# Emitting the five instruction streams directly instead of inside a block scope

## The chip, the cores and the metric

The kernel runs on one core of a Trainium2 chip. The metric is the device time of one execution in microseconds. It is a little longer than the span that the profile shows, which goes from the first to the last instruction of the program: the runtime's own work around the program counts in the time and not in the span. This document calls the difference "time minus span". Spans are listed to 0.1 us, so a single value carries up to 0.05 us of rounding. The means do not depend on it much, and for profiled runs the trace gives the span to a nanosecond.

## The reference, cut to what matters

Two branches on the same normalised input are added to that input: a diagonal state-space layer (a projection in, a complex recurrence over 2048 time steps, a projection out) and a dense layer with a Mish activation.

```
x = A_x                                  # 1 x 2048 x 1024, bf16
xn = layernorm(x)
return x + ssm(xn, Lambda, B, C, log_dt, Dskip) + mish(xn @ w1 + b1) @ w2     # w1: 1024 x 3584
```

The change touches none of this arithmetic.

## The kernel before

The kernel records every operation in one of five queues, one for each engine, with the semaphore waits that it needs. At the end the queues are emitted. An operation is emitted as its waits, then the instruction, which increments a semaphore:

```
    def emit(self, engine):
        known = {}
        for fn, waits, sem, inc in self.items:
            for ev in waits:
                if known.get(id(ev.sem), 0) < ev.val:
                    known[id(ev.sem)] = ev.val
                    engine.wait_ge(ev.sem, ev.val)
            if fn is not None:
                fn(engine).then_inc(sem, inc)
```

The last work of the program is an addition on DVE and an output transfer that ACT issues. SP (SyncE) waits for all output transfers, and this is the last entry of its queue:

```
            vop(lambda e: e.tensor_tensor(xr, src, xr, op=ALU.add), reads=b_src + [b_x], writes=[b_x])
            ...
            out_events[i, q, lo] = AC.dma(lambda e: e.dma_start(out[0, r0:r0 + P, lo:hi], xr), sem, reads=[b_x])
    ...
    SP.wait(out_events.values())

    with nc.Block() as block:
        @block.gpsimd
        def _(eng):
            PO.emit(eng)
        ...                                   # the same for vector, scalar, tensor
        @block.sync
        def _(eng):
            SP.emit(eng)
```

The block scope puts each engine's instructions into a block of its own, with a branch into it and a branch out of it, and ends with a barrier of all engines: each engine drains and counts up one semaphore, POOL waits for the four others and releases them through a second one. A barrier of the same kind stands at the program's start. That one belongs to the program's frame and not to the block.

## Time and profile before

| | before |
|---|---|
| time, median of 6 runs (range) | 624.51 us (624.31 to 625.04) |
| span of the profiled run | 622.4 us |
| PE busy | 616.7 us, 99% |
| time minus span, 25 runs of before with the later experiments | 1.99 us (1.94 to 2.02) |

From the page of the kernel before: the span, the busy time of each engine, and the chain of work that ended last, by engine and by line.

```profile
span 622.4 us, 7441 instructions
...
PE 616.7 (99%) x2981; PEld 287.9 (46%) x2981; DVE 464.1 (75%) x684; ACT 246.7 (40%) x162; POOL 50.2 (8%) x47
...
PE 98%; DMA 1%; DVE 1%; ACT 0%; SPq 0%; issue 0%
PE ps L715 49%; PE ps L638 29%; PE ps L658 18%; PE ps L492 2%; DMA xx<-in_A_x_dram 1%; DVE mt L663 0%; PE ps L378 0%; ACT sq L349 0%; SPq L287 0%; DVE xx L752 0%; ACT xnT L389 0%; DVE xn L366 0%; ACT mv L351 0%; ACT rs L360 0%; DVE rs L365 0%
```

The chain is matmuls for 98% of the span, and what lies after the last addition, 2.2 us of the span and about 2.0 us outside it, is 0.7% of the time. No more than that can be won at the program's end. The next lines are the end of the program in the timeline (start, length, engine, line, operation):

```profile
618.89 1.64 ACTq L754 DMA_DIRECT2D out_dram<-xx  x2
619.46 0.69 DVE L752 TENSOR_TENSOR xx<-ps,xx 128x512 bf16<-128x512 f32 x1 [0.60 <-PE ps L715]
```

The last addition on DVE ends at 620.15 us, but the span ends at 622.4. The views of the profile leave out drains, semaphores and branches, so for these 2.2 us one has to read the raw records of the trace. Here they are for the kernel before (start in us, length in ns; line 131 is the wait in `emit`, line 820 the block):

```
620.183   339 ns  ACT   DMA issue, the last output transfer   L754
621.893           last of the 16 landing counts of that transfer
621.910    28 ns  SP    semaphore wait, last of its queue but one  L131
621.977    41 ns  SP    compare-and-branch, carries the last wait  L820
622.158    13 ns  SP    drain                                 L820
622.196    17 ns  POOL  gathers four engines                  L820
622.274    17 ns  POOL  releases them                         L820
622.327    51 ns  PE    leaves; 622.378 is the end of the span  L820
```

So 0.485 us of the span lie after the last landing. After the span the records show updates of semaphore 2. The Trainium skill ("Runtime: NRT & Kernel Launch", Semaphores 0–2 are reserved) names it as the runtime's sync barrier. There are two passes of nine updates, and between them the user semaphores are set back to zero. In the kernel before, the first pass runs from 0.239 to 1.052 us after the span's end, the resetting ends at 1.604 (623.98 us), and the second pass runs from 1.859 to 2.215.

### The profile page before, as it was taken

The page shows a single profiled execution, that of the slowest core. Times are in us where ns is not written, and L with a number is a line of the kernel's source. Part 1 is how long each engine was busy: PE and PEld are TensorE (multiplying, and loading weights), DVE is VectorE, ACT ScalarE, POOL GpSimd, SP SyncE. Part 2 cuts the span into 40 slices and gives each one's busy share as a digit, 9 for nine tenths or more (in the row PEclk, how much of TensorE's full clock was granted, in tenths as well). Part 3 has the DMA queues.
Part 4 walks back from the last instruction along what each step waited for, and adds up shares of the span by engine and source line. Part 5 has one row for each costly group of instructions (what it writes and reads, how often), then busy time and mean ns, then how long its engine had stood idle before and what let it go on. Part 6 is the DMA issues. An engine that isn't in the chain of part 4 may idle for free.

```text
span 622.4 us, 7441 instructions
## 1 busy us (share of the span) xinstructions
PE 616.7 (99%) x2981; PEld 287.9 (46%) x2981; DVE 464.1 (75%) x684; ACT 246.7 (40%) x162; POOL 50.2 (8%) x47
## 2 busy tenths in 40 slices
PE   8999999999999999999999999999999999999998
PEld 7644444444444444444444444444444444444443
DVE  5799999999557599998147759999624856999603
ACT  6679995341069940000008992000001999000000
POOL 1999000000100000000010000000000000000000
PEclk9999999999999999999999999999999999999999
DMA  9999966750364300863055420285204531043001
GB/s 264 235 296 263 213 134 198 191 153 1 128 195 150 135 2 28 205 195 113 17 186 157 148 102 1 89 216 162 77 34 136 168 135 70 0 136 101 1 0 68
DMA packets 124188, 79.41 MB, mean 128 GB/s; under 512 B 48890, under 2 KB 106490, under 8 KB 124154
## 3 DMA queue, kind: packets, MB, share of 16 engines
q1 hardware_dynamic: 120656, 71.58, 42.5%
q10 hardware_dynamic: 2538, 4.21, 1.8%
q0 software_dynamic: 960, 3.15, 1.5%
q8 instruction: 24, 0.39, 0.3%
q14 instruction: 10, 0.08, 0.0%
HBM read 63.19 MB, written 4.19 MB: 108 GB/s over the span
## 4 chain that ended last, share of the span: by engine, by line
PE 98%; DMA 1%; DVE 1%; ACT 0%; SPq 0%; issue 0%
PE ps L715 49%; PE ps L638 29%; PE ps L658 18%; PE ps L492 2%; DMA xx<-in_A_x_dram 1%; DVE mt L663 0%; PE ps L378 0%; ACT sq L349 0%; SPq L287 0%; DVE xx L752 0%; ACT xnT L389 0%; DVE xn L366 0%; ACT mv L351 0%; ACT rs L360 0%; DVE rs L365 0%
## 5 line engine op out<-in xcount | busy, mean ns | idle before, releaser
L715 PE MATMUL ps<-ring,act 128*128 128x512 bf16 x896 | 194.2, 379 | 0.3 <-DVE mt L663 0.3
L638 PE MATMUL ps<-xnT,ring 128*128 128x512 bf16 x848 | 183.7, 379 | 0.0
L616 ACT ACTIVATE act<-hb 128x3584 bf16<-128x3584 bf16 x16 | 50.9, 3183 | 245.5 <-DVE hb L645 245.2
L715 PEld LDWEIGHTS ps<-ring,act 128*128 128x128 bf16 x896 | 87.6, 98 | 106.2 <-DVE mt L663 0.8
L638 PEld LDWEIGHTS ps<-xnT,ring 128*128 128x128 bf16 x848 | 83.0, 98 | 99.9
L645 DVE TENSOR_SCALAR hb<-ps,par 128x512 bf16<-128x512 f32 x112 | 82.8, 747 | 56.3 <-PE ps L638 54.4
L715 PE MATMUL ps<-CT,hT 128*128 128x512 bf16 x512 | 111.2, 379 | 0.0
L658 PE MATMUL ps<-xnT,BT 128*128 128x512 bf16 x512 | 111.2, 379 | 0.0
L663 DVE TENSOR_TENSOR mt<-ps,tab 128x1024 bf16<-128x1024 f32 x64 | 75.3, 1218 | 13.3 <-PE ps L658 11.8
L658 PEld LDWEIGHTS ps<-xnT,BT 128*128 128x128 bf16 x512 | 50.1, 98 | 60.4
L715 PEld LDWEIGHTS ps<-CT,hT 128*128 128x128 bf16 x512 | 50.1, 98 | 60.4
L752 DVE TENSOR_TENSOR xx<-ps,xx 128x1024 bf16<-128x1024 f32 (+1 forms) x17 | 19.5, 1159 | 70.3 <-PE ps L715 70.2
L681 DVE TENSOR_TENSOR_SCAN hT<-cs,qi,hT 128x512 bf16<-128x512 f32 x48 | 58.9, 1267 | 0.0
L618 ACT ACTIVATE act<-act 128x3584 bf16<-128x3584 bf16 x16 | 51.0, 3190 | 0.2
L617 ACT ACTIVATE act<-act 128x3584 bf16<-128x3584 bf16 x16 | 51.0, 3190 | 0.2
L686 DVE TENSOR_TENSOR mt<-hT,tab 128x1024 bf16<-128x1024 bf16 x64 | 41.4, 688 | 1.1
L623 DVE TENSOR_TENSOR act<-act,hb 128x3584 bf16<-128x3584 bf16 x16 | 32.9, 2058 | 1.3 <-ACT act L618 1.3
L287 POOL DMA_DIRECT2D xx<-in_A_x_dram x12 | 6.7, 559 | 254.0 <-DVE xx L752 249.9
L592 ACT ACTIVATE ct<-CT,cs 128x512 f32<-128x512 bf16 x16 | 11.5, 718 | 28.8 <-DVE CT L594 24.5
L617 ACT ACT_TABLE_LOAD x16 | 20.5, 1283 | 0.3
L618 ACT ACT_TABLE_LOAD x16 | 20.5, 1283 | 0.3
L681 DVE TENSOR_TENSOR_SCAN hT<-cs,hT 128x512 bf16<-128x512 f32 x16 | 18.7, 1207 | 0.0
(78 smaller groups left out, 277.2 us busy)
## 6 DMA issues: line engine op xcount, KB each, us to landing
ring<-in_B_w_dram SPq DMA_DIRECT2D x112, 512.0 KB, 3.7
out_dram<-xx ACTq DMA_DIRECT2D x15, 256.0 KB, 2.0
xx<-in_A_x_dram POOLq DMA_DIRECT2D x12, 256.0 KB, 4.1
xx<-in_A_x_dram SPq DMA_DIRECT2D x4, 256.0 KB, 3.6
dsk<-in_A_Dskip_dram SPq DMA_DIRECT2D x1, 256.0 KB, 6.7
out_dram<-xx ACTq DMA_DIRECT2D x2, 128.0 KB, 1.7
xnT<-xn SPq DMA_TRANSPOSE x12, 4.4
BT<-in_A_B_re_dram SPq DMA_TRANSPOSE x8, 5.7
```

Source lines behind the costliest of these rows:

```text
L616: aop(lambda e: e.activation(a, hs, AF.Exp), reads=[b_hb[g % 2]], writes=[b_act[g]])
L617: aop(lambda e: e.activation(a, a, AF.Ln, bias=1.0), reads=[b_act[g]], writes=[b_act[g]])
L618: aop(lambda e: e.activation(a, a, AF.Tanh), reads=[b_act[g]], writes=[b_act[g]])
L623: vop(lambda e: e.tensor_tensor(a, a, hs, op=ALU.mult), reads=[b_act[g], b_hb[g % 2]], writes=[b_act[g]])
L638: PE.mm(lambda e, k=k: e.matmul(ps[:, bank, :], lhsT=wt[:, k, fi * P:(fi + 1) * P], rhs=xnT[:, k, :], start=k == 0, stop=k == NK - 1), rea ...
L645: vop(lambda e: e.tensor_scalar(hb[:, hs, :], ps[:, bank, :], b1(f), None, op0=ALU.add), reads=[b_ps[bank], b_par], writes=[b_hbf[hs]])
L658: PE.mm(lambda e, j=j, ci=ci, k=k, bank=bank: e.matmul(ps[:, bank + ci, :], lhsT=BT[:, ci, j, k, :], rhs=xnT[:, k, :], start=k == 0, stop= ...
L663: vop(lambda e, s=s, u=u, j=j: e.tensor_tensor(mt[:, s, :, :], u, tab[:, s, j, :].unsqueeze(1).to_broadcast([P, 2, TB]), op=ALU.mult), rea ...
L681: vop(lambda e, ci=ci, init=init: e.tensor_tensor_scan(out=hT[:, ci, j, :], data0=cj("r", j).to_broadcast([P, TB]), data1=hT[:, ci, j, :], ...
L686: vop(lambda e, s=s: e.tensor_tensor(mt[:, s, :, :], hT[:, :, j, :], tab[:, s, j, :].unsqueeze(1).to_broadcast([P, 2, TB]), op=ALU.mult), ...
L715: PE.mm(lambda e: e.matmul(ps[:, u, :], lhsT=lhsT, rhs=rhs, start=st_, stop=last), reads=reads, writes=[b_ps[u]], first=st_, last=last)
L752: vop(lambda e: e.tensor_tensor(xr, src, xr, op=ALU.add), reads=b_src + [b_x], writes=[b_x])
```

## The change

The intent is to save the branches and the closing barrier, which the program does not need: SP has waited for every output transfer by then, and the runtime has a barrier of its own.

```diff
-    with nc.Block() as block:
-        @block.gpsimd
-        def _(eng):
-            PO.emit(eng)
...
-        @block.sync
-        def _(eng):
-            SP.emit(eng)
+    PO.emit(nc.gpsimd)
+    VE.emit(nc.vector)
+    AC.emit(nc.scalar)
+    PE.emit(nc.tensor)
+    SP.emit(nc.sync)
```

## The prediction

> **What bounds the kernel.** TensorE. The page shows PE busy 616.7 of a span of 622.4 us (99%) at granted clock 1.000; the chain that ended last is 98% PE. The time, 624.6 us (624.42 to 625.04), is 2.2 us longer than the span: work around the program.
>
> **What the change touches.** By the programs' instruction order, every compute and DMA instruction stays in place. Taken away are ten unconditional branches (into and out of each engine's block) and a closing barrier of five drains and six semaphore instructions. The opening barrier comes from the program, not from the block, and stays.
>
> **Branches: almost nothing.** The trace's raw records hold one branch, on SP at 621.98 us (41 ns; it carries the last semaphore wait); the nine others go to the next instruction and leave no record. At the start SP's release from the opening barrier stands at 0.708 us and its first DMA issue at 0.791, 83 ns later; two waits of SP in a row, without a branch, stand 67 ns apart: at most 16 ns. The Trainium skill ("Advanced Engine Details and Errata", Control Flow Timing) gives about 51 ns for a branch; the 83 ns leave no room for that. The start should not move: first DMA issue at 0.79, first matmul at 1.41.
>
> **Closing barrier: about 0.44 us of the span.** In the records the last output DMA lands at 621.89; SP's last ordinary wait ends at 621.94; branch 621.98; SP's drain 622.16; POOL gathers 622.20 and releases 622.27; the last engine leaves at 622.38, the span's end. Without the barrier SP's last wait ends the program: 622.38 - 621.94 = 0.44 us, all serial after the last DMA, so it counts in full. The other engines come early (DVE's drain ends 620.20, ACT's 620.72) and wait only for SP.
>
> **Outside the span: perhaps another 0 to 0.3 us.** After the span the records show updates of semaphore 2, which the Trainium skill ("Runtime: NRT & Kernel Launch", Semaphores 0–2 are reserved) names as the sync barrier: nine from 622.62 to 623.43, then the user semaphores cleared[...], then nine more from 624.24 to 624.59. The second pass takes 0.36 us, the first 0.81, because some engine comes late. With the change four engines arrive early and only SP late, so the first pass may come nearer to 0.36 (an estimate).
>
> **Sum.** 624.6 - 0.44 - about 0.15 = 624.0 us; -0.1%. The runs of before spread over 0.62 us, as much as the gain, so I give 623.4 to 624.6. Faster by over 2%: 1%; within 2%: 98%; slower by over 2%: 1%.
>
> **What would show it.** Span about 621.9 us instead of 622.4; last record an SP wait, 0.05 us after the last DMA lands; no drains or semaphores at the block's line; busy times, group means, idle times and first microseconds unchanged; PE chain still 98%. First pass of semaphore 2 earlier and shorter; the reset stage as long as before.
>
> **What would make it wrong.** (1) The runtime's end is set by something other than SP's arrival (an instruction block of 8192 bytes is fetched at 624.00): 0, or some tenths either way, since each engine's stream is now shorter. (2) Engines that enter the runtime's end early disturb the last output DMA or SP. (3) The block's barrier did part of the runtime barrier's waiting, and the gain is taken back there. (4) Run-to-run drift of some 0.3 us hides it.

## More of the kernel before

While the first rows are loaded and normalised, TensorE runs 76 dummy matmuls, so that its clock is up when the real work begins:

```
    keep_busy(76)
    ...
    first_apply(0)          # DVE: normalise rows 0..127
    first_transpose(0)      # PE: the first real work, after the dummies in PE's queue
```

## The result

The changed kernel took 623.77 us, median of 6 runs (623.34 to 624.32), against 624.51 us (624.31 to 625.04). The ratio is 0.9986 with a 95% interval of 0.9973 to 0.9999: faster by about 0.14%. Ratios in this document are the mean time of one kernel's fast runs over that of the other's of the same rounds, so they are not quite the ratio of the medians.

From the page of the changed kernel, the lines that answer to those of before:

```profile
span 622.6 us, 7430 instructions
...
PE 617.8 (99%) x2981; PEld 289.3 (46%) x2981; DVE 464.5 (75%) x684; ACT 246.7 (40%) x162; POOL 50.2 (8%) x47
...
PE 99%; DVE 0%; ACT 0%; POOL 0%; issue 0%; POOLq 0%
PE ps L715 48%; PE ps L638 29%; PE ps L658 18%; PE ps L492 2%; PE ps L457 1%; DVE mt L663 0%; PE ps L378 0%; DVE xx L752 0%; ACT xnT L389 0%; POOL ident L325 0%; POOL ident L324 0%; PE ps L500 0%; POOL kon L328 0%; POOLq L838 0%
```

Here is a trap. The profiled run of the changed kernel has a longer span than that of before (622.6 against 622.4), although the change took instructions away. The end of the timeline shows that the changed program was already late before its end came:

```profile
618.83 1.24 PE L715 MATMUL ps<-CT,hT 128*128 128x512 bf16 x5
...
620.11 0.69 DVE L752 TENSOR_TENSOR xx<-ps,xx 128x512 bf16<-128x512 f32 x1 [0.60 <-PE ps L715]
```

The last addition starts at 620.11 us instead of 619.46, so 0.65 us came in earlier. The chain has a clue: line 457, the dummy matmuls, is on it now (1%), and the load of the input is not. The start of the chain in order of time (start, length, what), first before, then after:

```profile
1.72 4.16 DMA xx<-in_A_x_dram
...
7.79 0.56 DVE xn L366
...
9.78 1.03 PE ps L492 x8
```

```profile
1.42 7.11 PE ps L457 x76
8.52 0.45 PE ps L378 x8
...
10.40 1.03 PE ps L492 x8
```

From the timelines, the dummies, the first normalised rows (DVE) and the first transposes (PE, line 378), first before, then after. The chain above counts a group on PE only from the end of the one before it, so it has the transposes at 8.52 us where the timeline has their start, 8.36:

```profile
1.41 5.65 PE L457 MATMUL ps<-ident 128*128 128x128 bf16 x76 [1.41 <-POOL kon L328]
...
6.83 0.55 DVE L366 TENSOR_SCALAR xn<-xx,mv,rs 128x1024 bf16<-128x1024 bf16 x1
...
7.43 0.62 PE L378 MATMUL ps<-ident,xn 128*128 128x128 bf16 x8 [0.36 <-DVE xn L366]
```

```profile
1.41 7.11 PE L457 MATMUL ps<-ident 128*128 128x128 bf16 x76 [1.41 <-POOL kon L328]
...
6.91 0.55 DVE L366 TENSOR_SCALAR xn<-xx,mv,rs 128x1024 bf16<-128x1024 bf16 x1
...
8.36 0.61 PE L378 MATMUL ps<-ident,xn 128*128 128x128 bf16 x8
```

And the durations of the dummy matmuls (min/median/max in ns), before and after:

```profile
L457 PE MATMUL ps<-ident x84: 219/219/311, 1.4 to 9.0; 128*128 128x128 bf16 x84
```

```profile
L457 PE MATMUL ps<-ident x84: 219/314/314, 1.4 to 9.6; 128*128 128x128 bf16 x84
```

In both kernels the dummies begin slow, 107 ns from start to start, and later quicken to 56 ns. In the run of before this happened at 4.11 us, in the run of the changed kernel at 7.19 us. The 76 dummies therefore last 7.11 us instead of 5.65, and the first transposes, which stand behind them in PE's queue, wait for them: they start at 8.36 us, although the first normalised rows were there at 7.45. The first real matmul (line 492, the dense layer) starts at 10.41 instead of 9.78 us.

The Trainium skill ("TensorE: Matmul & The Clock Gate", What's actually happening) says that the matmul clock is released after a busy window, and that the window is free-running, so that the moment varies from run to run. The traces agree that it varies: in the twelve profiles with 76 dummies the clock rose between 4.11 and 7.32 us, and in the ten of them without the block alone between 4.86 and 7.32. Only two of the twelve have the block, and they were early (4.11 and 5.29), so the profiles cannot show that the block has no part in the moment. Over all runs no difference stands out of the noise: the span less its tail after the last landing (measured once for each kernel) is on average 622.18 us in 47 runs without the block and 622.09 in 30 with it, a difference of 0.09 with a standard error of 0.08. From the first real matmul to the last matmul of the program, on the other hand, eleven of the twelve profiles lie between 609.26 and 609.31 us (the other, the run `e5_hold_pe`, at 609.90: at 93.5 us PE waits 0.91 us for DVE there, and 0.31 in the profile of `e7_hold_pool`). So the middle of the program is the same in all kernels but for one such stop. What differs is the start, which is chance as far as these runs can tell, and the end, which is the change.

The end of the changed kernel, from the raw records:

```
620.830   338 ns  ACT   DMA issue, the last output transfer   L754
622.537           last of the 16 landing counts of that transfer
622.554    28 ns  SP    semaphore wait, the last instruction of the program   L131
622.582           end of the span
```

The span's tail after the last landing is 0.045 us instead of 0.485: 0.44 us less. Time minus span fell as well, from 1.99 to 1.43 us (mean of 6 runs, 1.39 to 1.47). The parts, in us from the end of the span, from the updates of semaphore 2:

| | last landing to end of span | first pass: start, end | second pass: start, end | POOL's step in the second pass |
|---|---|---|---|---|
| before | 0.485 | 0.239, 1.052 | 1.859, 2.215 | 0.039 |
| changed | 0.045 | -2.337, 0.283 | 1.069, 1.621 | 0.233 |

From the last landing to the last update it is 2.700 us before and 1.666 us after, 1.03 us less. That is what the change is worth in these two traces. The difference of the mean times of the 6 and 6 runs is 624.62 - 623.76 = 0.85 us; the chance of the start lies on top (the spans of 25 runs of before have a standard deviation of 0.33 us).

### The profile page after: what moved, and what is told of

Read it like the earlier page. It is cut to its first block, busy times and chain, and to the rows that moved or that the text cites. A ratio compares the mean times of both kernels' runs of the same rounds, so it can differ in the third digit from the quotient of the medians.

```text
span 622.6 us, 7430 instructions
## 1 busy us (share of the span) xinstructions
PE 617.8 (99%) x2981; PEld 289.3 (46%) x2981; DVE 464.5 (75%) x684; ACT 246.7 (40%) x162; POOL 50.2 (8%) x47
## 4 chain that ended last, share of the span: by engine, by line
PE 99%; DVE 0%; ACT 0%; POOL 0%; issue 0%; POOLq 0%
PE ps L715 48%; PE ps L638 29%; PE ps L658 18%; PE ps L492 2%; PE ps L457 1%; DVE mt L663 0%; PE ps L378 0%; DVE xx L752 0%; ACT xnT L389 0%; POOL ident L325 0%; POOL ident L324 0%; PE ps L500 0%; POOL kon L328 0%; POOLq L838 0%
```

## The experiments

Theory: the time lost to the closing barrier has two parts. Inside the span it is the branch, drain, gather and release after SP's last wait. Outside the span it is that all engines come to the runtime's own barrier together, whereas without the closing barrier four of them have long been there and only SP is awaited. Rivals: the branches and the block as such; the length of the instruction streams, which moves what the runtime's instructions stand next to; and that the outside part is only noise. All twelve kernels gave the reference's result. The times of before are of the same rounds.

### e1_direct_barrier: the barrier without the block

```diff
     SP.emit(nc.sync)
+    nc.all_engine_barrier()
```

> The changed kernel (direct emission, no block) with one all-engine barrier put back at its end. Theory: the block's branches cost nothing and the barrier costs everything, so this is the kernel before again: time about 624.5 us like before in the same rounds (within 0.2), time minus span back at about 2.0 us (1.4 in the changed kernel), last landing to the end of the span about 0.4 to 0.5 us (0.485 before, 0.045 after). Rival (branches or block scope matter): part of the gain stays, time about 624.1 or less.

Measured: 624.33 us (623.78 to 624.95) against 624.49; ratio 0.9994 (0.9982 to 1.0007). Time minus span is 1.98 us (before 1.99), so the outside part is the barrier's alone. The tail of the span is 0.296 us, between the changed kernel's 0.045 and the 0.485 of before. SP's last wait stands at 622.207 and its drain at 622.272, 65 ns later. In the kernel before, the branch at 621.977 stands between them and the drain comes at 622.158, 181 ns after the branch. So the 0.44 us of span splits into 0.25 us for the barrier (0.296 - 0.045) and 0.19 us for the one branch of SP that carries a wait (0.485 - 0.296). The theory that branches cost nothing fell for that one. The times alone do not resolve 0.19 us.

### e2_hold_all: no barrier, but all five engines wait for the last transfers

```diff
     SP.wait(out_events.values())
+    for held in (PO, VE, AC, PE):
+        held.wait(list(out_events.values())[-2:])
```

> The changed kernel, but POOL, DVE, ACT and PE each also wait at their end for the last two output transfers, as SP does: no barrier, but all five engines reach the runtime's own end together. Theory: the gain outside the span comes from four engines doing their part of the runtime's end early, so it is lost here: time minus span about 2.0 us instead of 1.4, while the span's tail stays short (last landing to the end of the span 0.05 to 0.15 us); time about 0.4 us under before, about 0.6 over the changed kernel. Rival (the outside gain comes from shorter streams or another cause): time minus span stays 1.4 us.

Measured: 624.83 us (624.05 to 624.87) against 624.49; ratio 1.0 (0.9986 to 1.0013). The tail is 0.079 us, as short as expected, and time minus span is 2.08 us. The outside gain is gone without any barrier: it is enough that the engines come late together. The first pass shows it directly: it ends 0.804 us after the span, and 0.283 in the changed kernel. The time itself did not come out 0.4 us under before as expected; ratio and interval do not tell 0.999 from 1. One thing does not add up fully: the last update of semaphore 2 came 1.959 us after the span in this trace, less than the 2.215 of before, while the time minus span of the profiled run is 1.96, nearly the 2.02 of before. In twelve of the fourteen traces time minus span is 0.18 to 0.19 us less than the distance of that update from the span's end; here it is equal, and in the run `e7_hold_pool` below it is 0.08 us more. In these two traces alone a fetch of instructions ends after the last update (2.270 and 2.347 us after the span), and time minus span is 0.31 and 0.30 us less than that. So the fetch may set the end there, but no run tests it.

### e3_two_barriers: the kernel before with a second closing barrier

```diff
             SP.emit(eng)
+
+    nc.all_engine_barrier()
```

> The kernel before with a second closing barrier after the block's. Theory: a barrier more costs only its own drain, gather and release inside the span, about 0.2 to 0.35 us (before: SP's drain at 622.16 to the last leave at 622.38 is 0.22), since the engines come together already; time minus span stays 2.0 us. Rival (each barrier costs the whole difference of about 0.85 to 1.03 us): the time rises by 0.85 or more.

Measured: 624.84 us (624.57 to 625.8) against 624.49; ratio 1.0005 (0.9992 to 1.0017). The times alone do not exclude the 0.85 us of the rival: the interval reaches to a loss of 1.06 us. The pieces of the trace do, as the sum below shows. But the expected split was wrong: the tail grew by 0.67 us (1.151), and time minus span fell to 1.77. In the second barrier POOL's gather stands at 622.252 and its release only at 622.674, 0.42 us later, where the first barrier has 0.08. POOL stalled there. In exchange POOL's way back in the runtime's first pass, which took 0.311 us in the kernel before, took 0.039. From the last landing to the last update it is 3.129 us against 2.700, so 0.43 us for the second barrier, half of what the rival asked for.

### e4_pad: as many instructions as before, but no barrier

Waits that are long satisfied are added at the end of each stream, so that the five streams have the lengths of before (PE 6135, DVE 732, ACT 227, POOL 66, SP 285 instead of 6133, 730, 225, 63, 283).

```diff
-    PO.emit(nc.gpsimd)
+    for q, eng, n in ((PO, nc.gpsimd, 6), (VE, nc.vector, 4), (AC, nc.scalar, 4), (PE, nc.tensor, 4)):
+        q.emit(eng)
+        for _ in range(n):
+            eng.wait_ge(s_x0[0].sem, 16)        # two of these become one instruction
...                                                # SP: the same before its last waits
```

> The changed kernel with satisfied waits at the end of each engine's stream, so that each engine has exactly as many real instructions as before (PE 6135, DVE 732, ACT 227, POOL 66, SP 285), but no barrier. Theory: length has no part in it; time minus span stays about 1.4 us, span tail as in the changed kernel, time equal to the changed kernel (about 0.8 us under before). Rival (stream length, where the last instruction block begins): time minus span back at about 2.0 us, and an instruction fetch after the span as in before.

Measured: 623.56 us (623.12 to 623.91) against 624.49; ratio 0.9981 (0.9969 to 0.9994). The rival falls: with the old lengths the time does not go back, although a fetch of instructions is recorded again (0.06 us after the span's end). But the theory's "no part in it" falls too: time minus span is 1.23 us, 0.2 less than the changed kernel's 1.43. The 0.2 lies in one place, the third step of the runtime's second pass: 0.038 us here, 0.233 in the changed kernel. A longer stream was quicker.

### e5 to e8: one engine held at a time

```diff
     SP.wait(out_events.values())
+    PE.wait(list(out_events.values())[-2:])      # e5; AC in e6, PO in e7, VE in e8
```

> The changed kernel with PE alone (beside SP) waiting for the last two output transfers. In the run that held all four, the first update of the runtime's first pass came 0.19 us after the span's end. If PE is the first of the pass, it now starts at 0.19 again and runs through five steps and back: its end at about 0.55 us after the span instead of 0.28, so time minus span about 1.7 us instead of 1.43. Rival (PE has no part in it): 1.43.

> The changed kernel with ACT alone (beside SP) waiting for the last two output transfers. If ACT is second of the pass: its first update early, the second about 0.2 us after the span's end, end of the pass at about 0.5, time minus span about 1.65 us. Rival: 1.43.

> The changed kernel with POOL alone (beside SP) waiting. The third update of the first pass came 0.52 us after the span in the run that held all four, 0.25 later than the pass's own step: one engine needs some 0.25 us more than the others from its last instruction to the pass. Theory: that is POOL, so the pass ends at about 0.8 us, time minus span about 1.95 us (most of the 2.0). If it is another engine: about 1.6 us or 1.43.

> The changed kernel with DVE alone (beside SP) waiting. If DVE is the fourth of the pass and as quick as PE, the pass ends at 0.4 us or so, time minus span 1.5 to 1.6 us; if DVE is the slow third, about 1.95 us and POOL's run stays near 1.5.

Measured, with the time of the update that the held engine delays, in us after the end of the span:

| run | median time (before in the same rounds 624.50) | ratio (interval) | time minus span | delayed update | end of first pass |
|---|---|---|---|---|---|
| changed kernel | (other rounds) | | 1.43 | SP: 5th, 0.119 | 0.283 |
| e5_hold_pe | 623.71 | 0.9990 (0.9975 to 1.0004) | 1.69 | 1st, 0.190 | 0.547 |
| e6_hold_act | 623.57 | 0.9986 (0.9969 to 1.0003) | 1.58 | 2nd, 0.108 | 0.431 |
| e7_hold_pool | 624.41 | 0.9996 (0.9981 to 1.0011) | 2.12 | 3rd, 0.537 | 0.821 |
| e8_hold_dve | 623.55 | 0.9983 (0.9968 to 0.9998) | 1.55 | 4th, 0.146 | 0.386 |

The pass goes PE, ACT, POOL, DVE, SP and back: in each run exactly the held engine's update is the first late one, and all before it are early. PE, ACT and DVE cost 0.12 to 0.26 us when held, POOL 0.69. POOL's update comes 0.537 us after its last instruction's end, where the others need 0.11 to 0.19. The time minus span with POOL alone held is that of the run with all engines held (2.12 and 2.08 us). Not all of POOL's 0.69 is its late update, though. Holding POOL also makes its stream one instruction longer, 64 instead of 63, and in the updates the loss is 0.54 us at the end of the first pass (0.821 against 0.283) but only 0.35 at the end of the second (1.971 against 1.621). The other 0.34 us lies after the last update, in the end that was not explained above. That the way back runs through the same engines in reverse is inferred, since no run delayed an engine there. SP, the last of the five before the way back, is the best engine to let wait for the outputs: the changed kernel has it so already.

### e9_pad_pool and e10_pad_others: whose length gave the 0.2 us

```diff
     PO.emit(nc.gpsimd)
+    for _ in range(6):
+        nc.gpsimd.wait_ge(s_x0[0].sem, 16)        # e9; e10 pads the four others instead
```

> The changed kernel with three satisfied waits more at the end of POOL's stream alone (66 real instructions as before, 63 in the changed kernel). The run with all five streams padded had time minus span 1.23 us where the changed kernel has 1.43; the 0.2 lies in POOL's step of the runtime's second pass (0.233 us against 0.038). Theory: it hangs on POOL's stream alone, so time minus span 1.23 here and that step about 0.04 us. Rival (another stream's length): 1.43 and 0.23.

> The counterpart: PE, DVE, ACT and SP padded to their lengths of before, POOL left at 63. Theory (POOL's stream alone): time minus span 1.43 us, POOL's step of the second pass about 0.23 us. Rival (another stream, SP's above all): 1.23 and 0.04.

Measured: e9 623.30 us (623.03 to 623.64) against 624.35, ratio 0.9981 (0.9969 to 0.9994), time minus span 1.21 us, POOL's step 0.038 us. e10 623.80 us (623.56 to 624.11), ratio 0.9989 (0.9976 to 1.0001), time minus span 1.41 us, POOL's step 0.217. It is POOL's stream alone, as the theory said. In all fourteen traces the step is 0.217 to 0.235 us in the five kernels whose POOL stream has 63 instructions, and 0.038 to 0.061 us in the nine with 64 to 69.

A reading that fits these traces, but that no run was made to test: POOL stalls once, at about the same place of its stream, a few instructions after the 63rd. In the run with two barriers (69 instructions) this falls between POOL's last gather and release, in the kernel before (66) on its way back in the first pass, in the changed kernel (63) in the second pass, and in the padded ones into the time in which POOL waits for SP anyway, where it costs nothing. The two runs with 64 instructions (POOL held) fit too: there one block of 51 semaphores (105 to 155, POOL's by this reading) begins to be reset 0.42 to 0.44 us after the first pass, where in the twelve other traces it is 0.06 to 0.11. So the stall lies after the way back there, and POOL's late update of 0.537 us is a different thing. A fetch of an 8192-byte instruction block is recorded near the end in all nine kernels with 64 or more, and in none of the five with 63. The stall is not a wait for that block: in the six traces in which the end of the stall can be seen, the fetch begins 0.65 to 0.81 us after it. What POOL waits for stays open.

### e11_best and e12_before_warm56: fewer dummy matmuls

```diff
-    keep_busy(76)
+    keep_busy(56)              # e11: on e9_pad_pool; e12: on the kernel before
```

> The changed kernel with POOL padded as in the run e9_pad_pool, and 56 dummy matmuls at the start instead of 76. In ten profiles so far the matmul clock rises at 4.1 to 7.3 us, and the first real matmul group waits for the end of the dummies where it rises after about 6 us. Theory: with 56 the dummies end by about 7.4 us at the latest, before the first normalised rows are there, so late rises cost nothing: spans 621.6 to 622.2 instead of 621.9 to 622.9, time minus span 1.23, time about 623.1 us, 1.4 under before. Rival (the dummies' count does not set the spread, or fewer of them leave the clock low for longer): spans spread as before or longer, time about 623.5 or more.

> The kernel before with 56 dummy matmuls instead of 76. Theory: the run-to-run spread of the span comes from the start and has nothing to do with the block: the spread narrows as in e11_best, time minus span stays 2.0 us, time about 624.2 us, and the difference to e11_best is 0.44 us of span and 0.76 outside, about 1.2 us in sum. Rival (the spread comes from elsewhere): the spans still range over 0.9 us or so.

Measured: e11 623.22 us (622.92 to 623.9), ratio 0.9981 (0.9967 to 0.9994), spans 621.7 to 622.7; e12 624.42 us (624.08 to 625.73), ratio 1.0003 (0.9990 to 1.0015), spans 622.1 to 623.7. Time minus span is 1.21 and 1.98 us, as expected. The spread did not narrow: most spans are short, but each kernel has one that is 0.7 us or more over the next. In the profiled run of e11 the dummies leave PE waiting for the rows, as intended (columns as in the other timelines):

```profile
1.41 4.83 PE L457 MATMUL ps<-ident 128*128 128x128 bf16 x56 [1.41 <-POOL kon L328]
...
7.45 0.62 PE L378 MATMUL ps<-ident,xn 128*128 128x128 bf16 x8 [1.20 <-DVE xn L366]
```

But the long runs were not the profiled ones, so their cause stays open. A stop in the middle, as in the profile of `e5_hold_pe` (0.6 us), is of nearly that size and is not excluded. 56 dummies are no gain: e11's ratio equals that of e9, which keeps 76. The difference between e12 and e11 in mean time is 624.66 - 623.27 = 1.39 us, of which 0.77 us is time minus span.

The best version is therefore the changed kernel with three more instructions at the end of POOL's stream: a ratio of 0.9981 to before, 0.19%. The two intervals (0.9986 and 0.9981) overlap, and it is the time minus span (1.21 against 1.43 us, ranges that do not touch) that shows it to be better.

## Why the prediction was right or wrong

- **The time: right.** 624.0 us was predicted with 623.4 to 624.6, and 623.77 measured. The range was wide enough to hold no change at all (624.51), so falling inside it proves little, and that the number came within 0.25 us has luck in it: the two traces give 1.03 us for the end against the 0.59 that I had put into the sum, and the chance of the start took part of the difference back. The small size and the reason for it, that all of this lies serially at the end of a program that PE bounds for 98%, hold.
- **"Closing barrier: about 0.44 us of the span": the size right, the name half wrong.** The tail fell from 0.485 to 0.045 us, 0.44 exactly. But e1 shows that only 0.25 us of it are the barrier and 0.19 us the branch of SP that carries a wait.
- **"Branches: almost nothing": right at the start, wrong at the end.** SP's first DMA issue is at 0.790 us after and 0.791 before, 83 ns after its release from the opening barrier in both. (The argument that I gave was weaker than that: the second of the "two waits in a row" 67 ns apart is the closing branch itself, which carries a wait.) The step that failed is that I costed SP's closing branch at its record of 41 ns, and put the 0.14 us that follow it down to the barrier. What an instruction costs here is read from the distance to the next one, not from its own length.
- **"Outside the span: perhaps another 0 to 0.3 us": the mechanism right, the size too small.** I put in 0.15 us; it was 0.56 (1.99 - 1.43). I took the first pass's 0.81 us to be 0.36 and one late engine. By the steps it is 0.36, plus 0.18 for POOL's late update on the way out (0.221 against 0.039), plus 0.27 for POOL's stall on the way back (0.311 against 0.038; that this step is POOL's is the reading given under e9). I left out that with four engines waiting already the pass has no way out left at all: after SP's update (0.119 us) only the way back remains, and it ends 0.283 us after the span instead of 1.052. That is a gain of 0.77, and 0.44 of it is SP's earlier update (0.561 to 0.119). Most of the rest is that stall, which by the same reading did not vanish but moved: 0.2 us was given back by POOL's step in the second pass, and the second pass as a whole came 0.02 us closer after the first.
- **"First microseconds unchanged", "span about 621.9": wrong for the profiled run.** Its span was 622.6, because the matmul clock rose at 7.19 us instead of 4.11. I had taken the start of a single trace for a property of the kernel. Over all runs it shows: four kernels without barrier and with nobody held (changed, e4, e9, e10; 21 runs) have a mean span of 622.28 us, 25 runs of before 622.58. The difference of 0.30 us, with a standard error of about 0.1 from the two spreads (0.31 and 0.33 us), agrees with 0.44 within the noise.
- **"What would make it wrong", (1), shorter streams: true as a term.** POOL's stream at 63 instructions cost 0.2 us in the runtime's second pass (e9 against e10). (4) was so in part: single spans hide the gain. (2) was not seen: the middle of the program is unchanged to 0.05 us between before and changed, and the last transfer lands 1.71 us after its issue before and after. (3) is answered by e2, e7 and e1: the block's barrier did not save the runtime's, it made its first pass longer.

## What to carry to other kernels

If one engine already waits for all outputs, as here, a closing barrier before the runtime's own one was paid twice: once for itself, and once because it sends all engines late into the next barrier, where otherwise only the waiting one would be late (the run that held all engines shows this without a barrier). Let the engine wait that comes last in that barrier's order (here SP) and never hold back the one that is slowest to come (here POOL). For effects under 1 us, compare pieces of the trace that repeat (last landing to end, first to last real matmul, time minus span) rather than two spans, since a change of the start by chance can hide them or pass for them.

## What the Trainium skill lacked or had wrong

- "Runtime: NRT & Kernel Launch", The ~15µs preamble/postamble breakdown: it gives 44 ns a hop times 8, about 355 ns, for the pass of the barrier before the kernel, and about 1.5 us for the barrier after it, described as a wait for all engines. An undisturbed pass here takes 0.356 us, which agrees (the steps run from 23 to 98 ns). But the first pass after the kernel ended 1.05 us after the program with a closing barrier and 0.28 us without. The page does not say how much of it depends on when each engine comes.
- The same page has no order of the engines: PE, ACT, POOL, DVE, SP, by the four runs that held one engine, and back (in reverse, as inferred). It also does not say that POOL needs 0.54 us from its last instruction to its update, where the others need 0.11 to 0.19.
- "Advanced Engine Details and Errata", Control Flow Timing: it gives about 51 ns for an unconditional branch. Nine of the ten branches of the block left no record in the trace and cost nothing that shows. The tenth, which carries a wait, appears as a compare-and-branch of 41 ns, but it is 181 ns from it to the next instruction, and with block and branch gone the tail is 0.19 us shorter. The page gives about 108 ns for a compare-and-branch.
- "TensorE: Matmul & The Clock Gate", Part 1: it gives a spread of plus or minus 500 ns for the moment at which the clock rises. Here it rose 2.7 to 5.9 us after the first matmul (4.11 to 7.32 us in the trace), a range of 3.2 us, which with 76 dummies moves the first real matmul between 9.51 and 10.48 us. The listed mean granted clock was 1.000 in these profiles and does not show it.
- No page has that three more instructions at the end of POOL's stream (66 instead of 63) take 0.2 us off the runtime's end (time minus span 1.21 instead of 1.43 us).
